# Chunk 4's last 64 keys share a bank with sums of values, in one matmul group

## The chip, the cores and the metric

The kernel runs on one core of a Trainium2 chip. The metric is the device time in microseconds; the kernel before has a median of 1121.96 us over three runs (1121.49 to 1125.24). A core has a matmul engine (TensorE, PE in the profile, with its weight loads as PEld), VectorE (DVE), ScalarE (ACT), GpSimd (POOL), and SyncE (SP), which issues the DMAs here. Matmuls write to PSUM, which has eight banks of 512 float32 columns in each of 128 partitions.

## The reference

Two stages follow each other: an attention whose mask is causal by blocks of 64, over 8 batches of 8 heads (576 positions, head size 64), and a gated feed-forward on its 4608 rows of 512 (hidden size 2048).

```python
scores = scale * np.matmul(q, k.transpose(0, 1, 3, 2))
mask = block_i >= block_j                  # blocks of 64 positions
attn = exp(scores - max); attn = attn / (sum(attn) + 1e-09)
x = np.matmul(attn, v)                     # then heads side by side: 4608 x 512
h = x @ w_in                               # 512 -> 2048
g = h * (1.0 / (1.0 + np.exp(-1.702 * h)))
out = g @ w_out                            # 2048 -> 512
```

## The kernel before

**Attention.** The kernel takes the heads two at a time: turn `n` of 32 works on pair `n`, the two heads of which lie in partitions 0 to 63 and 64 to 127. `prep` (L292) turns q and k on VectorE into `qk`. The 576 queries of a head form five chunks: chunk 0 has 64 queries, chunks 1 to 4 have 128 each, and chunk `i` sees the first 64(2i+1) keys, which is 576 for chunk 4. `score` (L305) multiplies a chunk's queries with its keys into PSUM banks, `weigh` (L340) takes masked scores out of a bank with a VectorE operation that also finds the maximum (L351) and applies the exponential on ScalarE (L358), `normalise` (L364) divides by the sum (GpSimd at L376, from turn 8 on VectorE for chunk 4 at L378), and `turn` (L382) transposes the weights on VectorE (L385, L390). After chunk 4 the turned weights are rearranged by 16 DMAs. `av` (L429) multiplies them with the values one turn later, so turn `n` holds the sums of values of pair `n`-1.

Chunk 4 is wider than a bank: 576 columns against 512. So `score` cuts its keys in two pieces, 0 to 255 and 256 to 575, each with a bank per head: four banks. With float32 each matmul shows as two records per head in the trace, and the two heads, in different halves of the array, run beside each other.

**Feed-forward.** It runs in float32r with every operand split in a high and a low part, so each product is three matmuls. A *step* of it, as the words below call it, is a tile of 384 rows with 128 of the 2048 hidden columns. Its first half is 12 matmuls into one bank (`hp`); then come the gate (tanh on ScalarE L562, a VectorE operation L563 that reads `hp` and writes `g`, a rounding on ScalarE L571, a subtraction on GpSimd L82). The second half is 9 matmuls into three banks (`acc`) and runs after the next step's first half. There is a single `hp` bank, so a first half can't begin before L563 of the step ahead of it is done.

**What sets the order.** `ORDER` (L26) has a string for each phase; its third string is for turns 9 to 31 (turn 8 has `HANDOVER`). An item is a group of chunks to score (`3+0/2+1`, `4`), `V` (the sums of values), `L` (`prep` of the next pair), or `-`. After each item, `advance` (L592) adds feed-forward steps up to a quota, from turn 9 on only whole ones, so a group of attention matmuls always stands after a first half. TensorE keeps this program order (L98, L101). On the other engines the framework's scheduler lays down a fixed order when the program is built, by data dependences and priorities (the gate has a raised one, L561 and L570), and each engine then takes its instructions strictly in that order.

Banks outside the feed-forward come from `bank()` (L89), which goes round w0 to w3 in these turns. Buffers `e0` and `e1` hold the weights of even and odd chunks.

Of the kernel before, what the change touches and what calls it, by code (L numbers as in the profile page):

```python
# [10 lines left out]
F32 = mybir.dt.float32  # L11
# [14 lines left out]
ORDER = (  # L26
# [3 lines left out]
)  # L30

START = "1+0 - B 2/3 L C - V - 4 - a - - -"
# [8 lines left out]
def attention_moe_kernel(  # L41
# [9 lines left out]
    nc = tc.nc  # L51
    B, H, S, D = q.shape
# [51 lines left out]

    ident = sp.tile([P, P], F32, name="ident")
    make_identity(nc, ident)
    MW = 448
    mask = sp.tile([P, MW], mybir.dt.bfloat16, name="mask")
    nc.gpsimd.memset(mask, 0.0)
    nc.gpsimd.memset(mask[0:BLK, MW - BLK : MW], -8e9)  # L110
# [16 lines left out]
        return home[name, g]  # L127

    xr = sp.tile([P, NDC, RING], F32, name="xr")


    vp = sp.tile([P, 2, NCH, D], F32, name="vp")
# [32 lines left out]
    def width(i):  # L165
        return BLK * (2 * i + 1)
# [125 lines left out]
    def prep(n):  # L292

        tag = "e0" if early(n) and n % 2 else "qk"
        qk[n] = d2.tile([P, 2, S], F32, tag=tag, name="qk", bufs=1)
        for x in range(2):
            nc.vector.transpose(out=qk[n][:, x], in_=raw[n][:, x].rearrange("p c d -> p (c d)"))  # L297
        raw.pop(n)
        m = follower(n)
        if m is not None:  # L300
            load(m)

    stats = {}

    def score(n, banks):  # L305

        if n not in stats:
            mx = d2.tile([P, NCH + 1, 2], F32, tag="mx", name="mx")
            sm = d2.tile([P, NCH, 2], F32, tag="sm", name="sm")
            stats[n] = (mx, sm)  # L310
        todo = []
        for chunks in banks:

            part = []
            for lo, hi in ((0, 512),) if width(chunks[0]) <= 512 else ((0, 256), (256, S)):
                ss = [bank() for _ in range(2)]
                c = 0
# [12 lines left out]
            todo.append(sorted(part, key=lambda x: (chunks[::-1].index(x[0]), x[2])))  # L330
        for chunks, part in zip(banks, todo):
            e = {}
            for i, hd, lo, hi, s in part:
                e[i] = weigh(n, i, hd, lo, hi, s, e.get(i))
            for i in chunks[::-1]:
                normalise(n, i, e[i])
                if not early(n):
                    turn(n, i, e[i])

    def weigh(n, i, hd, lo, hi, s, e):  # L340
# [10 lines left out]
        nc.vector.tensor_tensor_reduce(  # L351
            out=e[0:m, hd, lo:hi], in0=s, in1=mk,
            op0=ALU.add, op1=ALU.min, scale=-0.125,
            scalar=3e38 if lo == 0 else mx[0:m, NCH, hd : hd + 1],
            accum_out=mx[0:m, i, hd : hd + 1] if hi == w else mx[0:m, NCH, hd : hd + 1],
        )
        if hi == w:
            nc.scalar.activation(  # L358
                out=e[0:m, hd], in_=e[0:m, hd], func=AF.Exp, scale=-1.0,
                bias=mx[0:m, i, hd : hd + 1], accum_out=sm[0:m, i, hd : hd + 1],  # L360
            )
        return e
# [63 lines left out]
                in_=src[:, x : x + 2 * len(part), a : a + 2],  # L426
            )

    def av(n):  # L429

        b, h = divmod(n, HP)
        before_av(n)
        o, o0 = bank(), bank()

        todo = []
        for i in range(1, NCH):
            c = (i - 1) * P
            todo += [(o, c, P, j, pw[:, :, SLOT[i] + j]) for j in range(i)]
            todo.append((o, c + BLK, BLK, i, pw[:, 2:4, 9 + i]))
        last = len(todo) - 1  # L440
        todo.append((o0, 0, BLK, 0, pw[:, 0:2, 10]))

        for x, (bk, c, nn, j, w) in enumerate(todo):
            for hd in range(2):
                mm(
                    out=bk[hd * D : hd * D + D, c : c + nn].rearrange("d (a c) -> d a c", c=32),
                    lhsT=values(n)[:, hd, j], rhs=w[:, :, hd], start=x in (0, last + 1), stop=x >= last,
                )
        c0 = (b % 2) * S
        nc.scalar.copy(out=xr[:, h, c0 : c0 + BLK], in_=o0[:, 0:BLK])  # L450
        nc.scalar.copy(out=xr[:, h, c0 + BLK : c0 + S], in_=o)
        m = follower(n)
        if m is not None:
            load_v(m)

    def follower(n):

        m = {0: 2, 1: 3, 2: 4, 3: None}.get(n, n + 1)
        return None if m is None or m >= NPAIR else m

    def order(n):
        return {HP: START, 2 * HP: HANDOVER}.get(n, ORDER[phase(n)]).split()

    def step(n):

        turns["n"] = n
        now = n < NPAIR

        def item(x):
            if x == "V":  # L470
                return (lambda: av(n - 1)) if n else None
            if x == "L":
# [33 lines left out]
    def chunk_time(tt):  # L506
        return 4 * unit1(tt) + tt // P * 650
# [69 lines left out]
        yield from second(prev)  # L577


    ends = np.cumsum([0.0] + [NFC * chunk_time(tt) for _, tt in TILES])  # L580

    def quota(pos):
        xs, ys = zip(*TILES_BY)
        return -1.0 if pos < xs[0] else np.interp(pos, xs, [ends[y if y >= 0 else y - 1] for y in ys])

    def heads_for(t):
        return -(-sum(TILES[t]) // S) * H
# [36 lines left out]
    for n in range(NPAIR + 1):  # L624
        items = step(n)
        for sl, fn in enumerate(items):
            if fn is not None:
                fn()
            if order(n)[sl] == "V":
# [35 lines left out]
```

## Time and profile before

| | before |
|---|---|
| median of 3 runs | 1121.96 us |
| profiled execution: own time | 1120.49 us |
| profiled execution: span of the instructions | 1118.6 us |
| TensorE busy | 1076.4 us (96%) |
| VectorE busy | 583.0 us (52%) |
| ScalarE busy | 498.6 us (45%) |
| GpSimd busy | 406.7 us (36%) |
| mean granted TensorE clock | 0.992 |

Turn 8 begins at about 192 us, the last group of chunk 4 is at 947 us, and behind it the feed-forward runs alone up to 1118.6 us. In the rows of the timeline, the first number is the start in us from the span's beginning, the second the time in us, then engine, line, operation, what it writes and reads, the shape and a count. Starts of matmuls tell more than their times: the next matmul starts while the one before it still drains, so the recorded times overlap.

### The profile page before, as it was taken

What the parts mean: (1) busy time and instruction counts of PE and PEld (TensorE: products, weight loads), DVE (VectorE), ACT (ScalarE), POOL (GpSimd) and SP (SyncE); (2) the same over time, 40 slices, a digit from 0 to 9 for tenths busy, and PEclk for the clock granted to TensorE, in tenths of its full rate; (3) what the DMA queues carried; (4) which work ended last, traced back from release to release, by engine and by line L of the source; (5) the groups of instructions that cost most, each with busy time, mean ns of one, the idle gap of its engine ahead of it and who ended that gap; (6) DMA issues with size and microseconds to landing.
All of it is one profiled execution on the core that took longest, in us unless ns stands there. A gap on an engine that the chain in (4) does not pass through costs nothing. (4 is left out here: it accounts for less than half of the span.)

```text
span 1118.6 us, 19977 instructions
## 1 busy us (share of the span) xinstructions
PE 1076.4 (96%) x6960; PEld 908.7 (81%) x6960; DVE 583.0 (52%) x1856; ACT 498.6 (45%) x1321; POOL 406.7 (36%) x509
## 2 busy tenths in 40 slices
PE   5969998999999999999999999999999999999998
PEld 3757776788888888888888888888888888899997
DVE  6776885545545555654555655645545654211210
ACT  5866776434534433534443543444434444322322
POOL 4665664333333332333333333333333233122222
PEclk9979999999999999999999999999999999999999
DMA  8734532332444432343443333344342332200000
GB/s 171 205 89 153 150 73 62 84 79 57 105 86 86 103 80 64 64 98 78 98 101 74 75 93 65 70 108 85 81 107 63 71 85 58 54 29 1 29 1 29
DMA packets 219365, 91.25 MB, mean 82 GB/s; under 512 B 197760, under 2 KB 197760, under 8 KB 219264
## 3 DMA queue, kind: packets, MB, share of 16 engines
q1 hardware_dynamic: 214528, 89.38, 34.0%
q10 hardware_dynamic: 4736, 0.59, 0.3%
q8 instruction: 55, 0.90, 0.3%
q14 instruction: 46, 0.38, 0.1%
HBM read 45.09 MB, written 9.44 MB: 49 GB/s over the span
## 5 line engine op out<-in xcount | busy, mean ns | idle before, releaser
L82 POOL TENSOR_TENSOR gl<-g,gh 128x384 fp32r<-128x384 f32 x192 | 194.7, 1014 | 551.5 <-ACT gh L571 449.1
L99 PE MATMUL hp<-xh,wih 128*128 128x384 f32 x768 | 264.7, 345 | 7.9 <-DVE g L563 6.9
L563 DVE SCALAR_TENSOR_TENSOR g<-g,hp 128x384 f32<-128x384 f32 x192 | 105.9, 552 | 319.1 <-ACT g L562 317.8
L99 PE MATMUL hp<-xh,wil 128*128 128x384 f32 x768 | 258.4, 336 | 0.1
L562 ACT ACTIVATE g<-hp 128x384 f32<-128x384 f32 x192 | 94.1, 490 | 359.8 <-PE hp L99 354.8
L99 PE MATMUL hp<-xl,wih 128*128 128x384 f32 x768 | 253.9, 338 | 0.4 <-DVE xl L82 0.4
L99 PE MATMUL acc<-woh,gh 128*128 128x512 f32 x576 | 233.9, 406 | 0.0
L99 PE MATMUL acc<-wol,gh 128*128 128x512 f32 x576 | 226.9, 394 | 0.0
L99 PEld LDWEIGHTS hp<-xh,wih 128*128 128x128 f32 x768 | 144.2, 188 | 34.1 <-DVE g L563 23.1
L99 PE MATMUL acc<-woh,gl 128*128 128x512 f32 x576 | 167.9, 393 | 0.3 <-POOL gl L82 0.3
L571 ACT CAST gh<-g 128x384 fp32r<-128x384 f32 x192 | 98.4, 513 | 156.5 <-DVE g L563 156.4
L99 PEld LDWEIGHTS hp<-xh,wil 128*128 128x128 f32 x768 | 144.3, 188 | 6.5 <-POOL wil L82 0.7
L358 ACT ACTIVATE e<-e,mx 64x64 f32<-64x64 f32 (+4 forms) x240 | 132.3, 552 | 37.6 <-DVE mx L351 37.6
L376 POOL TENSOR_TENSOR e<-e,sm 64x64 f32<-64x64 f32 (+1 forms) x192 | 113.6, 612 | 95.0 <-DVE sm L371 46.5
L99 PEld LDWEIGHTS hp<-xl,wih 128*128 128x128 f32 x768 | 143.6, 188 | 1.3 <-DVE xl L82 1.3
L99 PE MATMUL bank<-qk 64*128 64x320 f32 (+4 forms) x768 | 122.5, 428 | 14.5 <-DVE qk L297 11.1
L99 PEld LDWEIGHTS acc<-woh,gh 128*128 128x128 f32 x576 | 107.9, 187 | 34.2 <-issue 10.5
L99 PEld LDWEIGHTS acc<-woh,gl 128*128 128x128 f32 x576 | 107.8, 188 | 25.9 <-POOL gl L82 1.2
L99 PEld LDWEIGHTS acc<-wol,gh 128*128 128x128 f32 x576 | 108.3, 188 | 16.7 <-POOL wol L82 0.3
L351 DVE CUSTOM_DVE_ANT_0 e<-bank,mask 64x64 f32<-64x64 f32 (+4 forms) x240 | 89.7, 417 | 56.9 <-PE bank L99 52.8
L385 DVE STREAM_TRANSPOSE turned<-e 128x384 f32<-128x384 f32 (+1 forms) x192 | 92.3, 499 | 48.8 <-POOL e L376 48.3
L99 PEld LDWEIGHTS bank<-qk 64*128 64x128 f32 x768 | 69.6, 193 | 54.2 <-issue 25.4
(50 smaller groups left out, 956.0 us busy)
## 6 DMA issues: line engine op xcount, KB each, us to landing
turned<-turned SPq DMA_DIRECT2D x192, 80.0 KB, 2.1
turned<-turned SPq DMA_DIRECT2D x96, 112.0 KB, 2.2
raw<-in_q_dram SPq DMA_DIRECT2D x128, 72.0 KB, 2.4
out_dram<-osb SPq DMA_DIRECT2D x36, 256.0 KB, 2.2
raw<-in_k_dram SPq DMA_DIRECT2D x120, 72.0 KB, 2.6
turned<-turned SPq DMA_DIRECT2D x96, 88.0 KB, 2.1
words<-in_moe_w_in_dram SPq DMA_DIRECT2D x16, 512.0 KB, 6.3
vp<-in_v_dram SPq DMA_DIRECT2D x60, 128.0 KB, 2.4
```

The costliest lines, as they stand in the source:

```text
L82: eng.tensor_tensor(out=out, in0=in0, in1=in1, op=ALU.subtract)
L99: return tc.keep_in_program_order(nc.tensor.matmul(**kw))
L351: nc.vector.tensor_tensor_reduce(out=e[0:m, hd, lo:hi], in0=s, in1=mk, op0=ALU.add, op1=ALU.min, scale=-0.125, scalar=3e38 if lo == 0 else ...
L358: nc.scalar.activation(out=e[0:m, hd], in_=e[0:m, hd], func=AF.Exp, scale=-1.0, bias=mx[0:m, i, hd : hd + 1], accum_out=sm[0:m, i, hd : hd ...
L376: nc.gpsimd.tensor_tensor(out=x, in0=x, in1=sc.to_broadcast([m, width(i)]), op=ALU.mult)
L385: nc.vector.transpose(out=tw[:, :, SLOT[i] : SLOT[i] + i, hd].rearrange("p b j c -> p j b c"), in_=e[:, hd, 0 : i * P],)
L562: nc.scalar.activation(out=g, in_=hp[:, 0:tt], func=AF.Tanh, scale=1.702)
L563: nc.vector.scalar_tensor_tensor(out=g, in0=g, scalar=1.0, in1=hp[:, 0:tt], op0=ALU.add, op1=ALU.mult)
L571: nc.scalar.copy(out=gh, in_=g)
```

## The change

- `ORDER`'s third string: `V` and `4`, which stood at items 5 and 8, become one item `V4` at item 9 of 13. So from turn 9 on, the sums of values of pair `n`-1 and chunk 4 of pair `n` are one group of matmuls with nothing between.
- That group needs four banks: two for the sums of values (`o`, `o0`), two for keys 0 to 511 of chunk 4, one per head. The last 64 keys of both heads go into columns 64 to 191 of `o0`, of which the sums of values use 64 columns. One matmul over all 128 partitions does both heads: `ends` holds the last keys of the two heads as a block diagonal with zeros elsewhere.
- `prep` writes keys 0 to 511 into `qk` and the last 64 into `ends`, by two more small transposes (for pairs 9 on).
- In `av` (all turns) chunk 0's matmuls, which fill `o0`, come first and not last.
- From turn 8 on, the weights of chunks 0 and 1 lie in a buffer of their own (`small`), no longer in `e0` and `e1`.

```diff
-    "3+0/2+1 - - - V - - 4 - - - L -",
+    "3+0/2+1 - - - - - - - V4 - - L -",
...
+    ends = sp.tile([P, 2, BLK], F32, name="ends")
+    nc.gpsimd.memset(ends, 0.0)
...
         for x in range(2):
-            nc.vector.transpose(out=qk[n][:, x], in_=raw[n][:, x].rearrange("p c d -> p (c d)"))
+            z = QC * P if x and n > 2 * HP else S
+            nc.vector.transpose(out=qk[n][:, x, 0:z], in_=raw[n][:, x, 0 : z // 32].rearrange("p c d -> p (c d)"))
+            for hd in range(2 if z < S else 0):
+                r = slice(hd * D, hd * D + D)
+                nc.vector.transpose(
+                    out=ends[r, hd], in_=raw[n][r, x, z // 32 : S // 32].rearrange("p c d -> p (c d)")
+                )
...
-            for lo, hi in ((0, 512),) if width(chunks[0]) <= 512 else ((0, 256), (256, S)):
+            cuts = (0, 512) if width(chunks[0]) <= 512 or shared is not None else (0, 256, S)
+            for lo, hi in zip(cuts, cuts[1:]):
...
+            if shared is not None:
+                i = NCH - 1
+                mm(
+                    out=shared, lhsT=qk[n][:, 0, slice(*qrange(i))], rhs=ends.rearrange("p h k -> p (h k)"),
+                    start=True, stop=True,
+                )
+                part += [(i, hd, QC * P, S, shared[:, hd * BLK : (hd + 1) * BLK]) for hd in range(2)]
...
-            e = d2.tile([P, 2, w], F32, tag=f"e{i % 2}", name="e", bufs=1)
+            if i > 1:
+                e = d2.tile([P, 2, w], F32, tag=f"e{i % 2}", name="e", bufs=1)
+            else:
+
+                if n not in small:
+                    small[n] = room("wm", [P, WC], F32, "e")
+                e = small[n][:, 2 * 3 * BLK * (1 - i) : 2 * (3 * BLK + w * (1 - i))].rearrange("p (h k) -> p h k", h=2)
...
+        todo.insert(0, (o0, 0, BLK, 0, pw[:, 0:2, 10]))
         last = len(todo) - 1
-        todo.append((o0, 0, BLK, 0, pw[:, 0:2, 10]))
...
+    def values_and_4(n):
+        o0 = bank()
+        av(n - 1, o0)
+        if n < NPAIR:
+            score(n, [[NCH - 1]], o0[:, BLK : 3 * BLK])
```

The places in the built order of which the next part speaks are these. On TensorE, turn 19: before, chunk 4 was a group between two halves of feed-forward steps.

```order
L99 MATMUL hp_5910<-xl_978,wih_187 128x384
L99 MATMUL bank_5930<-qk_5655 128x256
L99 MATMUL bank_5931<-qk_5655 128x256
L99 MATMUL bank_5934<-qk_5655 128x320
L99 MATMUL bank_5935<-qk_5655 128x320
L99 MATMUL acc0_5869<-woh_410,gh_5886 128x512
```

In the changed kernel, the same turn has the end of the sums of values (bank 5875; chunk 0's are in 5874), then chunk 4 with the shared bank.

```order
L99 MATMUL bank_5875<-turned_77,vp_75 64x128 x8
L99 MATMUL bank_5875<-turned_77,vp_75 64x64 x2
L99 MATMUL bank_5912<-qk_5636 128x512
L99 MATMUL bank_5913<-qk_5636 128x512
L99 MATMUL bank_5874<-ends_73,qk_5636 128x128
L99 MATMUL acc0_5813<-woh_412,gh_5830 128x512
```

The two groups have become one, with five matmuls behind the sums of values where four stood alone.

On VectorE, turn 19, from the last score piece of chunk 4 to the first of turn 20: before, the two transposes of `prep` (`qk`, L297, q and k) stand ahead of chunk 4's scaling (L378) and transposes (L385, L390), and the gates of the two steps behind chunk 4 (`g_5990`, `g_6031`) come last.

```order
L351 ISA e_5938,mx_5696<-bank_5935,mask_69,mx_5696 128x320
L351 ISA mx_5696 128x1
L297 STREAM_TRANSPOSE qk_5997<-raw_5658 128x576 x2
L368 TENSOR_SCALAR sm_5697<-sm_5697 128x2
L371 RECIPROCAL sm_5697<-sm_5697 128x2
L378 TENSOR_SCALAR e_5938<-e_5938,sm_5697 128x576 x2
L385 STREAM_TRANSPOSE turned_75<-e_5938 128x4x4x32 x2
L390 STREAM_TRANSPOSE turned_75<-e_5938 64x2x2x32
L563 SCALAR_TENSOR_TENSOR g_5990<-g_5990,hp_5977 128x384
L563 SCALAR_TENSOR_TENSOR g_6031<-g_6031,hp_6018 128x384
```

In the changed kernel (lines of the new file: L302 and L305 are `prep`'s transposes, L599 is the gate, L404, L411 and L416 are chunk 4's scaling and transposes), the same stretch:

```order
L302 STREAM_TRANSPOSE qk_5976<-raw_5641 128x576
L394 TENSOR_SCALAR sm_5680<-sm_5680 128x2
L397 RECIPROCAL sm_5680<-sm_5680 128x2
L404 TENSOR_SCALAR e_5917<-e_5917,sm_5680 128x576 x2
L411 STREAM_TRANSPOSE turned_77<-e_5917 128x4x4x32 x2
L599 SCALAR_TENSOR_TENSOR g_5969<-g_5969,hp_5956 128x384
L416 STREAM_TRANSPOSE turned_77<-e_5917 64x2x2x32
L305 STREAM_TRANSPOSE ends_73<-raw_5641 64x64
L599 SCALAR_TENSOR_TENSOR g_6012<-g_6012,hp_5999 128x384
L302 STREAM_TRANSPOSE qk_5976<-raw_5641 128x512
L305 STREAM_TRANSPOSE ends_73<-raw_5641 64x64
```

The transpose of k (`qk_5976` 128x512) has moved from ahead of chunk 4's scaling to behind the gate `g_6012` of the second step after chunk 4. On TensorE, that step's first half (`hp_5999`) stands right before the first scores of turn 20, which read `qk_5976`.

```order
L99 MATMUL hp_5999<-xh_979,wil_190 128x384
L99 MATMUL hp_5999<-xl_980,wih_189 128x384
L99 MATMUL bank_6021<-qk_5976 128x448
L99 MATMUL bank_6022<-qk_5976 128x448
L99 MATMUL bank_6021<-qk_5976 128x64
```

Of the 22 turns 9 to 30, twelve have the transpose of k behind the gate of the last first half before the next turn's scores, as here (13, 16, 18, 19, 20, 21, 23, 24, 26, 27, 28, 29); in the other ten it stands ahead of that gate.

More of the change, by code (lines that the diff above doesn't have):

```diff
@@ L106, in attention_moe_kernel @@
     make_identity(nc, ident)
-    MW = 448
+    MW = 576
     mask = sp.tile([P, MW], mybir.dt.bfloat16, name="mask")
@@ L303, in attention_moe_kernel, with score @@
     stats = {}
-    def score(n, banks):
+    def score(n, banks, shared=None):
         if n not in stats:
@@ L338, in score @@
                     turn(n, i, e[i])
+    small = {}
     def weigh(n, i, hd, lo, hi, s, e):
@@ L427, in flip, with av @@
             )
-    def av(n):
+    def av(n, o0=None):
         b, h = divmod(n, HP)
         before_av(n)
-        o, o0 = bank(), bank()
+        o = bank()
+        if o0 is None:
+            o0 = bank()
         todo = []
@@ L446, in av @@
                     out=bk[hd * D : hd * D + D, c : c + nn].rearrange("d (a c) -> d a c", c=32),
-                    lhsT=values(n)[:, hd, j], rhs=w[:, :, hd], start=x in (0, last + 1), stop=x >= last,
+                    lhsT=values(n)[:, hd, j], rhs=w[:, :, hd], start=x in (0, 1), stop=x in (0, last),
                 )
@@ L459, in follower @@
         return None if m is None or m >= NPAIR else m
+    def values_and_4(n):
+        o0 = bank()
+        av(n - 1, o0)
+        if n < NPAIR:
+            score(n, [[NCH - 1]], o0[:, BLK : 3 * BLK])
     def order(n):
@@ L471, in item @@
                 return (lambda: av(n - 1)) if n else None
+            if x == "V4":
+                return lambda: values_and_4(n)
             if x == "L":
@@ L577, in moe @@
         yield from second(prev)
-    ends = np.cumsum([0.0] + [NFC * chunk_time(tt) for _, tt in TILES])
+    tile_ends = np.cumsum([0.0] + [NFC * chunk_time(tt) for _, tt in TILES])
     def quota(pos):
         xs, ys = zip(*TILES_BY)
-        return -1.0 if pos < xs[0] else np.interp(pos, xs, [ends[y if y >= 0 else y - 1] for y in ys])
+        return -1.0 if pos < xs[0] else np.interp(pos, xs, [tile_ends[y if y >= 0 else y - 1] for y in ys])
     def heads_for(t):
@@ L628, in attention_moe_kernel @@
                 fn()
-            if order(n)[sl] == "V":
+            if order(n)[sl][0] == "V":
                 heads_done = 2 * n
```

## The prediction

> **What bounds the kernel now.** I read the page, then the busy times by stage, then who waits for whom on TensorE in the stage that changes, and last the timelines around the groups that move.
>
> ```profile
> PE 1076.4 (96%) x6960; PEld 908.7 (81%) x6960; DVE 583.0 (52%) x1856; ACT 498.6 (45%) x1321; POOL 406.7 (36%) x509
> ```
> ```profile
> 236.00:950.00 714.00, 708.62 (x4628) 600.88 (x4627) 392.02 (x1299) 299.46 (x807) 239.24 (x310) 1.00 0.37 82
> ```
> ```profile
> PE hp L99 <- DVE g L563: 5.1, 6, 0.9
> ```
>
> From 236 to 950 us, where turns 9 to 31 run, TensorE (first of the busy times) is busy for 708.6 of 714 us at full granted clock, and the wait view of this stretch has one entry: six waits for the gate's VectorE operation. So TensorE's chain sets the end. What the change is worth there is the matmul time it saves, the waits it removes, and the waits it makes. Other engines cost something only when TensorE waits for them. Before 236 us the order of the groups on TensorE stays, and from 950 us on it runs the feed-forward alone; I put no change there.
>
> **Term A, one group in place of two (turns 9 to 31, 23 times).** Rows of TensorE around chunk 4 and around the sums of values, turn 18:
>
> ```profile
> 526.87 0.34 PE L99 MATMUL hp<-xl,wih 128*128 128x384 f32 x1
> 527.14 1.24 PE L99 MATMUL bank<-qk 64*128 64x256 f32 x8
> ...
> 527.67 0.70 PE L99 MATMUL bank<-qk 64*128 64x320 f32 x4
> ...
> 527.94 0.44 PE L99 MATMUL bank<-qk 64*128 64x320 f32 x2
> ...
> 528.31 0.50 PE L99 MATMUL acc<-woh,gh 128*128 128x512 f32 x1
> 528.65 0.39 PE L99 MATMUL acc<-wol,gh 128*128 128x512 f32 x1
> ```
> ```profile
> 515.54 2.99 PE L99 MATMUL bank<-turned,vp 128*64 128x128 f32 x60
> 518.45 0.50 PE L99 MATMUL acc<-woh,gh 128*128 128x512 f32 x1
> 518.79 0.40 PE L99 MATMUL acc<-wol,gh 128*128 128x512 f32 x1
> 519.03 0.39 PE L99 MATMUL acc<-woh,gh 128*128 128x512 f32 x1
> ```
>
> Starts tell the cost. The last 384-column matmul holds the next start off by 0.27 us (526.87 to 527.14), where within a half they follow each other after 0.18 (further below, eleven of them from 502.68 to 504.70): 0.10 to enter a group, rounded up. The first matmul behind a group takes 0.34 (528.31 to 528.65, 518.45 to 518.79) against 0.24 for the next (518.79 to 519.03): 0.10. A pass over 320 columns takes 0.27 (527.67 to 527.94), 0.84 ns per column, both heads side by side. Chunk 4 has two passes over 576 columns, 0.97 us, but lasts 1.17 (527.14 to 528.31): 0.20 more, a second weight load that nothing covers and the drain at the end. The values' group lasts 2.91 us with its own drain.
>
> Before, a turn spends 0.10 + 2.91 + 0.10 on V and 0.10 + 1.17 + 0.10 on chunk 4: 4.48 us. After, 0.10 + 2.91, then two passes of 512 columns (0.86) with 0.20 as before, then the shared matmul's two passes of 128 (0.22). For the shared matmul's second load and the step back to the feed-forward no row exists: nothing at the cheapest, 0.25 at the dearest (0.10 twice and 0.05). I take 0.07, nearer to the low end, since the feed-forward has the same 128 by 128 shape. Sum 4.36: 0.12 less, 2.8 us in 23 turns, with bounds of 4.4 saved and 1.4 lost.
>
> Two sentences of the Trainium skill stand beside this. Its page "TensorEngine Tiling (Array Packing)", section "Key Properties", says that a change of tiling mode drains the engine; the rows agree (0.10 on entry), and by that rule alone the way back costs nothing, which would make the saving 4.4 us. Its page "TensorE: Matmul & The Clock Gate", Part 3 on packing small matmuls, says that matmuls in different row groups run at once and that one over all rows takes as long as a small one; it speaks against this change, since 128 columns at full height take the place of 64 side by side, 0.11 us a turn or 2.5 us in all by the pass row above.
>
> **Term B, the wait for the gate behind chunk 4 goes.** Two turns, early and late, and an undisturbed half for comparison:
>
> ```profile
> 244.19 0.86 PE L99 MATMUL acc<-woh,gl 128*128 128x512 f32 x3
> 245.88 0.45 PE L99 MATMUL hp<-xh,wih 128*128 128x384 f32 x1 [0.82 <-DVE g L563]
> ```
> ```profile
> 501.82 0.86 PE L99 MATMUL acc<-woh,gl 128*128 128x512 f32 x3
> 502.68 0.45 PE L99 MATMUL hp<-xh,wih 128*128 128x384 f32 x1
> ```
> ```profile
> 519.95 0.84 PE L99 MATMUL acc<-woh,gl 128*128 128x512 f32 x3
> 520.62 0.33 PE L99 MATMUL hp<-xh,wih 128*128 128x384 f32 x1
> ```
>
> Undisturbed, the half starts 0.67 us after the three matmuls begin; in the early turn after 1.69, in the late one after 0.86. So six early turns lose 1.0 us each and some fifteen late ones 0.19 (with about 0.05 more at the half ahead of chunk 4): 9.6 us in all. The reason stands on VectorE, where chunk 4's chain is ahead of the gate (turn 17; chunk 4 starts on TensorE at 494.98):
>
> ```profile
> 494.98 0.49 PE L99 MATMUL bank<-qk 64*128 64x256 f32 x2
> ```
> ```profile
> 495.71 0.42 DVE L351 CUSTOM_DVE_ANT_0 e<-bank,mask 128x256 f32<-128x256 f32 x1 [3.09 <-PE bank L99]
> ...
> 496.87 0.55 DVE L351 CUSTOM_DVE_ANT_0 e<-bank,mask,mx 128x320 f32<-128x320 f32 x1
> ...
> 497.81 1.43 DVE L297 STREAM_TRANSPOSE qk<-raw 128x576 f32<-128x576 f32 x2
> 499.17 0.13 DVE L368 TENSOR_SCALAR sm<-sm 128x2 f32<-128x2 f32 x1
> ...
> 500.40 1.30 DVE L385 STREAM_TRANSPOSE turned<-e 128x512 f32<-128x512 f32 x2
> 501.73 0.31 DVE L390 STREAM_TRANSPOSE turned<-e 64x128 f32<-64x128 f32 x1
> 502.07 0.55 DVE L563 SCALAR_TENSOR_TENSOR g<-g,hp 128x384 f32<-128x384 f32 x1
> ```
> ```profile
> 497.46 0.78 ACT L358 ACTIVATE e<-e,mx 128x576 f32<-128x576 f32 x1 [0.30 <-DVE mx L351]
> ```
> ```profile
> L351 DVE CUSTOM_DVE_ANT_0 e<-bank,mask 128x448 f32<-128x448 f32 x48 | 27.7, 610 | 0.0
> ```
>
> I rebuild this chain for the changed order, counting from the group's first score matmul. The first score operation comes at 0.73 now, and at 0.73 + 0.43 = 1.16 with 512 columns (two passes of 256 more). 256 columns take 0.42, 448 take 0.61: about 1 ns a column, so 512 take 0.67 and follow each other after 0.60; the 64-column piece is 0.27 (0.55 less 256 columns). The first exponential starts 0.05 behind the end of its head's last piece: 1.16 + 1.20 + 0.27 + 0.05 = 2.68. From there to the sums (L368) it is 1.71 (497.46 to 499.17): 4.39. From the sums to the gate it is 2.90, less the 0.34 of L390, which the new order puts behind the gate: gate from 6.95 to 7.50. TensorE would begin that half, without a wait, at 502.68 - 494.98 - 0.19 = 7.51 now, and at 7.6 behind the longer group. So the gate is just in time. The moved transposes of `prep` fill VectorE's wait for the exponentials, and the gate of the step before runs beside the 2.9 us of V. I take 8.0 us saved, with 1.6 left for what is late by a hair; bounds are 3 (the chain 0.3 longer each turn) and 9.6.
>
> **Term C, a new wait: the first scores of the next turn.** The order shows it: in 12 of 22 turns the transpose of k stands behind the gate of the half that runs right before the scores that read it. Before, that transpose was done far ahead (497.81 in the turn above, seven us before the scores). The price comes from the rows at such a place:
>
> ```profile
> 504.70 0.34 PE L99 MATMUL hp<-xl,wih 128*128 128x384 f32 x1
> 504.97 2.11 PE L99 MATMUL bank<-qk 64*128 64x448 f32 x16
> ```
> ```profile
> 505.13 0.49 ACT L562 ACTIVATE g<-hp 128x384 f32<-128x384 f32 x1 [1.97 <-PE hp L99]
> ```
> ```profile
> 505.65 0.56 DVE L563 SCALAR_TENSOR_TENSOR g<-g,hp 128x384 f32<-128x384 f32 x1 [3.04 <-ACT g L562]
> ```
> ```profile
> L385 DVE STREAM_TRANSPOSE turned<-e 128x512 f32<-128x512 f32 x48 | 31.1, 687 | 0.0
> ```
> ```profile
> 57.88 0.75 DVE L297 STREAM_TRANSPOSE qk<-raw 128x576 f32<-128x576 f32 x1
> ```
> ```profile
> 58.69 0.43 PE L99 MATMUL bank<-qk 64*128 64x192 f32 x2 [2.52 <-DVE qk L297]
> ```
>
> The half's last matmul starts at 504.70 and the scores at 504.97. The tanh can't start before 505.13, the gate before 505.65; it ends at 506.21, a 512-column transpose (0.69, the nearest form) at 506.90, and TensorE goes on 0.06 behind such a transpose (58.63 to 58.69): 506.96. That is 1.99 late, or 1.90 if the two VectorE operations overlap as others do by 0.09. VectorE idles 3 us before this gate, so nothing shortens it, and behind the waiting scores stand all later matmuls, since TensorE keeps its order. 12 times 1.95 is **23.4 us lost**. The bounds are 19.5 (two of the twelve places harmless) and 26 (2.2 us each, should another 0.2 lie between the links); TensorE waits for nothing else there that could hide it.
>
> **Term D, small moves.** In turn 16 the new order has three transposes of GpSimd-scaled weights ahead of the first gate behind the scores.
>
> ```profile
> L376 POOL TENSOR_TENSOR e<-e,sm 128x448 f32<-128x448 f32 x48 | 43.8, 933 | 14.2 <-DVE sm L371 13.5 <-ACT e L358 0.7
> L376 POOL TENSOR_TENSOR e<-e,sm 128x320 f32<-128x320 f32 x48 | 33.6, 720 | 29.1 <-DVE sm L371 29.1
> L376 POOL TENSOR_TENSOR e<-e,sm 128x192 f32<-128x192 f32 x48 | 23.3, 507 | 33.9 <-ACT e L358 33.9
> ```
> ```profile
> 509.28 1.83 POOL L376 TENSOR_TENSOR e<-e,sm 128x448 f32<-128x448 f32 x2 [0.47 <-DVE sm L371]
> ```
>
> Two of each are 4.3 us. Before, the first began 4.3 us behind the scores' start (504.97 to 509.28); with the scores of chunks 1 and 2 now ahead of its sums on VectorE I take 5.0. With a transpose (0.31) and the gate (0.55) the bank is free at 10.2; TensorE needs it behind the scores (2.1) and three halves of 2.1, at 8.4: 1.8 us lost, once. The two extra transposes per turn and the DMAs for the next pair, which SyncE issues behind the transpose of k, have most of a turn (some 30 us) to land in, so they cost nothing unless that shrinks below the time of a transfer.
>
> **Sum.** -2.8 - 8.0 + 23.4 + 1.8 = +14.4 us on the profiled execution's 1120.5 (span 1118.6), so 1134.9. The median shown is 1.5 above that execution: **1136.5 us**.
>
> **Rivals.** (1) *Faster: the wait of term C is not paid.* If the scores wait less than (2.8 + 8.0 - 1.8) / 12 = 0.75 us a turn, the kernel gains; at nothing it comes to 1113. For it: the trace of before has no such wait. Against: VectorE takes instructions in the order of the rows, and the gate needs a half that TensorE has only just finished. (2) *The gains cancel it:* the wait at 0.75 us gives 1122, no change; it needs most of the 12 places to be harmless. (3) *Term B brings nothing,* the chain being 0.35 longer than I rebuilt: 1144.5. (4) *The shared matmul waits for ScalarE,* which must first copy chunk 0's sums out of the same bank (the order has that copy ahead of the gate's rounding, some 3 us before it is needed). If it came late by 0.5 us a turn, 1148.
>
> **How the numbers follow.** Forecast 0.68; rival 1 0.12; rival 2 0.06; rival 3 0.08; rival 4 0.06. A measurement tells about 0.3% (3.4 us) from no change. Slower holds the forecast and rivals 3 and 4, 0.82; within 0.3% 0.06; faster 0.12. The range leaves out rival 1 below, and what is dearer than 1147 above: 1124 to 1147.
>
> **What would show it.** In the new profile, TensorE should wait for `qk` (L302) about 12 times for 1.5 to 2 us each between 330 and 900 us, and the six waits for the gate should be gone; the group V with chunk 4 should last about 4.2 us. I am wrong if the wait view has no entry for `qk`, if the time stays under 1124, or if waits for ScalarE stand at the shared matmul.

## The result, and the profile after

| kernel | median us (range, runs) | against the kernel before, 95% interval |
|---|---|---|
| before | 1123.60 (1121.49 to 1125.28, 4) | |
| changed | 1139.72 (1139.47 to 1140.05, 4) | 1.0148 [1.0128, 1.0168] |

The changed kernel is slower by 1.5%, 16 us; its profiled span is 1138.1 us where that of before is 1118.6. The forecast of 1136.5 us lies 3.2 us below the median.

The page's first part (busy time, share of the span, instructions) and the windows view of the stretch with turns 9 to 31 in the changed kernel:

```profile
PE 1075.2 (94%) x6914; PEld 915.9 (80%) x6914; DVE 597.6 (53%) x1902; ACT 500.9 (44%) x1321; POOL 403.6 (35%) x510
```
```profile
236.00:970.00 734.00, 708.66 (x4665) 609.64 (x4664) 407.28 (x1346) 302.96 (x811) 236.84 (x310) 1.00 0.36 80
```

TensorE has no more work than before (1075 us against 1076), and in this stretch as much busy time as before (708.7 against 708.6 us), but the stretch holds 25 us in which it idles, where there were 5.4. What it waits for is in the wait view of the same stretch (who waits for whom: us in all, times, longest):

```profile
PE bank L99 <- DVE qk L302: 23.8, 12, 2.2
PE hp L99 <- DVE g L599: 1.4, 1, 1.4
```

The six waits for the gate have become one, and twelve waits for the transpose of k have come in. One of the twelve, ahead of turn 17, in the timeline (start, duration, engine, instruction, idle time before it and its releaser):

```profile
476.48 0.34 PE L99 MATMUL hp<-xl,wih 128*128 128x384 f32 x1
476.91 0.49 ACT L598 ACTIVATE g<-hp 128x384 f32<-128x384 f32 x1 [1.47 <-PE hp L99]
477.43 0.56 DVE L599 SCALAR_TENSOR_TENSOR g<-g,hp 128x384 f32<-128x384 f32 x1 [2.42 <-ACT g L598]
477.90 0.71 DVE L302 STREAM_TRANSPOSE qk<-raw 128x512 f32<-128x512 f32 x1
478.76 1.51 PE L99 MATMUL bank<-qk 64*128 64x448 f32 x10 [1.94 <-DVE qk L302]
```

From the half's last matmul to the scores it is 478.76 - 476.48 = 2.28 us, where 0.27 is the step without a wait: 2.01 us lost. VectorE did nothing for 2.42 us ahead of the gate; the transpose needed nothing of it and only stood behind it.

How far the changed kernel is behind the one before, by the start of each turn's first scores in the two traces:

| turn | 4 | 6 | 7 | 8 | 9 | 16 | 17 | 24 | 31 | end |
|---|---|---|---|---|---|---|---|---|---|---|
| us behind | 1.7 | 0.5 | 4.8 | 6.6 | 6.6 | 2.4 | 6.0 | 13.1 | 20.3 | 19.5 |

Two things stand in it. From turn 10 on the kernel gains 0.4 to 1.2 us in a turn without the wait, and loses 1.0 to 2.1 net in a turn with it (3.6 in turn 16). And 6.6 us were lost before turn 9, where I had put no change.

### The profile page after: what moved, and what is told of

It reads as the page before. It is cut to its first block, busy times and chain, and to the rows that moved or that the text cites. A ratio compares the mean times of both kernels' runs of the same rounds, so it can differ in the third digit from the quotient of the medians.

```text
span 1138.1 us, 19974 instructions
## 1 busy us (share of the span) xinstructions
PE 1075.2 (94%) x6914; PEld 915.9 (80%) x6914; DVE 597.6 (53%) x1902; ACT 500.9 (44%) x1321; POOL 403.6 (35%) x510
## 4 chain that ended last, share of the span: by engine, by line
PE 50%; DVE 3%; DMA 2%; ACT 2%; issue 1%; SPq 1%; POOL 0%; POOLq 0%; DVEq 0%; ACTq 0%
PE hp L99 21%; PE acc L99 21%; PE bank L99 9%; DMA turned<-turned 2%; ACT e L384 1%; SPq L423 1%; DMA vp<-in_v_dram 1%; DVE e L404 1%; DVE qk L302 1%; DVE g L599 1%; DVE turned L411 1%; DVE e L377 0%; DVE sm L394 0%; DVE sm L397 0%; ACT g L598 0%
## 5 line engine op out<-in xcount | busy, mean ns | idle before, releaser
L599 DVE SCALAR_TENSOR_TENSOR g<-g,hp 128x384 f32<-128x384 f32 x192 | 105.5, 549 | 372.6 <-ACT g L598 372.2
L99 PE MATMUL bank<-qk 64*128 64x320 f32 (+5 forms) x676 | 119.3, 454 | 37.0 <-DVE qk L302 31.0
L377 DVE CUSTOM_DVE_ANT_0 e<-bank,mask 64x64 f32<-64x64 f32 (+5 forms) x240 | 103.2, 463 | 56.2 <-PE bank L99 55.8
L99 PEld LDWEIGHTS bank<-qk 64*128 64x128 f32 x676 | 62.3, 194 | 70.3 <-issue 46.5
L99 PEld LDWEIGHTS bank<-turned,vp 128*64 128x64 f32 x1800 | 86.9, 139 | 13.1 <-issue 6.4
```

What stands on the lines that cost most here:

```text
L99: return tc.keep_in_program_order(nc.tensor.matmul(**kw))
L377: nc.vector.tensor_tensor_reduce(out=e[0:m, hd, lo:hi], in0=s, in1=mk, op0=ALU.add, op1=ALU.min, scale=-0.125, scalar=3e38 if lo == 0 else ...
L599: nc.vector.scalar_tensor_tensor(out=g, in0=g, scalar=1.0, in1=hp[:, 0:tt], op0=ALU.add, op1=ALU.mult)
```

## The experiments

Ten kernels ran. Numbers in brackets are the 95% interval of the ratio to the kernel before, whose median in these comparisons was 1123.2 to 1123.6 us.

| run | median us (range) | ratio | behind the kernel before at turn 9 / 31, us |
|---|---|---|---|
| 1 k ahead | 1123.8 (1119.9 to 1126.0) | 1.0006 [0.9993, 1.0020] | 9.5 / 6.4 |
| 2 early order | 1138.2 (1133.3 to 1140.9) | 1.0128 [1.0095, 1.0161] | 1.1 / 19.9 |
| 3 pins only | 1163.0 (1162.0 to 1164.9) | 1.0356 [1.0333, 1.0379] | 8.4 / 42.7 |
| 4 both | 1117.2 (1116.6 to 1119.1) | 0.9947 [0.9930, 0.9963] | 2.6 / -0.6 |
| 5 before, chunk 0 first | 1132.2 (1132.0 to 1134.1) | 1.0080 [1.0066, 1.0094] | 11.8 / 11.8 |
| 6 more waits taken out | 1114.0 (1113.1 to 1116.2) | 0.9915 [0.9901, 0.9930] | 1.2 / -5.3 |
| 7 shared matmul twice | 1121.5 (1118.6 to 1123.6) | 0.9984 [0.9973, 0.9995] | -0.3 / -1.2 |
| 8 groups apart, 4 turns | 1119.8 (1117.2 to 1120.0) | 0.9959 [0.9944, 0.9974] | 2.7 / 0.4 |
| 9 groups apart | 1117.9 (1116.0 to 1119.0) | 0.9949 [0.9934, 0.9964] | -0.2 / -3.8 |
| 10 gate later | 1122.2 (1121.7 to 1124.9) | 0.9993 [0.9981, 1.0005] | 1.3 / 3.2 |

### 1. The transpose of k ahead of the last gate

```diff
-    "3+0/2+1 - - - - - - - V4 - - L -",
+    "3+0/2+1 - - - T - - - V4 - - L -",
...
+            if z < S:
+                tc.keep_in_program_order(d)
...
+                    if turns["n"] > 2 * HP:
+                        tc.keep_in_program_order(d)
```

`d` is the transpose of k in the first place and the gate's VectorE operation in the second; a third pin, not shown here, is on the transpose of chunk 4's tail. The scheduler may no longer exchange these. `T` issues the transposes of the turn's scaled weights at that slot, and `L` the transpose of chunk 4's tail with its DMAs, so that the other operations keep their places.

> The changed kernel with one thing moved: in every turn from the tenth on, the transpose of the next pair's k stands ahead of the gate of the turn's last half on VectorE (chunk 4's turned transposes and its tail's transpose with its 16 DMAs go to other places in the turn, so that the rest of VectorE's order stays). Theory (the late transpose of k is the loss): the waits of TensorE for qk (L302) after 236 us, 24.7 us in 12 turns by the starts, go and nothing takes their place: 1139.7 - 24.7 = 1115, between 1112 and 1119. Rival (the wait only moves: the scores, or a half shortly behind, then wait for the gate or for another VectorE operation): 1130 or more, with a new entry of 1 us a turn in the waits.

Measured 1123.8, between the two. The wait view from 236 us on:

```profile
PE hp L99 <- DVE g L627: 4.8, 3, 2.1
PE bank L99 <- DVE qk L302: 3.5, 2, 1.7
```

Ten of the twelve waits are gone. Two are left, where VectorE has four other operations ahead of the transpose (run 6). By starts, 24.7 us of waits for qk have become 3.6. Against this stand two halves that wait longer (turn 9 by 1.4, turn 13 by 1.65 us, both of this edit's order), 2.9 us that this run lost by turn 9 beside the changed kernel, and 3.4 us at half clock in turn 9, which cost 1.7. All halves together are 2.8 us later. From the changed kernel's span this makes 1138.1 - 21.1 + 2.8 + 2.9 + 1.7 = 1124.4 us, and the span of this run is 1124.2. So the waits were on the path, and their removal was paid in full; I had counted as if none were left and none came.

### 2 and 5. Chunk 0's matmuls last or first in the early turns

Run 2 is the changed kernel with this in `av`; run 5 is the kernel before with the reverse.

```diff
-        todo.insert(0, (o0, 0, BLK, 0, pw[:, 0:2, 10]))
+        first = (o0, 0, BLK, 0, pw[:, 0:2, 10])
...
+        if n < 2 * HP:
+            todo.append(first)
...
+        else:
+            todo.insert(0, first)
```

> The changed kernel, in which the sums of values of the first eight pairs again have chunk 0's matmuls last, as before the change. Theory (the 6.5 us that the changed kernel had lost by turn 8 come from this order, through the engines behind it): 1139.7 - 6.5 = 1133, between 1131 and 1135. Rival (they come from where stretches of half clock happened to fall in the first 210 us, and the order of these matmuls is worth nothing): 1139 to 1141.

> The kernel before, in which the sums of values of the first eight pairs have chunk 0's matmuls first, as in the changed kernel; nothing else of the change is in it. Theory (this order alone makes the early loss: it was worth 6.6 us between the runs with k's transpose ahead): 1123.2 + 6 = 1129, between 1127 and 1132, and in the trace turn 9's scores start about 5 us later than before. Rival (the loss is of other stretches of the run, or of where half clock falls by chance): 1122 to 1125.

Run 2's trace is 5.4 us ahead of the changed kernel's at turn 9, but its time does not tell: four executions took 1133.3 to 1140.9 us, and their median of 1138.2 lies between the two expectations. Its profile lost 5 us again later. The same wait for qk, ahead of turn 14's scores, in the changed kernel and in run 2, in the timeline and in the windows view of two stretches each (the third number from the right is the granted clock):

```profile
383.81 2.11 PE L99 MATMUL bank<-qk 64*128 64x448 f32 x16 [1.94 <-DVE qk L302]
```
```profile
379.18:382.59 3.41, 2.68 (x14) 2.06 (x13) 2.55 (x7) 1.00 (x2) 1.01 (x1) 1.00 0.10 22
382.59:386.00 3.41, 2.19 (x17) 1.60 (x18) 2.31 (x10) 1.25 (x6) 0.99 (x1) 1.00 0.64 153
```
```profile
378.35 3.79 PE L99 MATMUL bank<-qk 64*128 64x448 f32 x16 [1.94 <-DVE qk L302]
```
```profile
375.15:378.56 3.41, 1.47 (x10) 1.18 (x10) 2.44 (x6) 1.00 (x2) 0.82 (x2) 1.00 0.36 85
378.56:381.98 3.42, 3.42 (x16) 2.18 (x14) 1.54 (x9) 1.39 (x7) 0.64 (x1) 0.50 0.57 134
```

The wait is the same, but in run 2 the scores behind it took 3.79 us and not 2.11: the clock had fallen to half for 3.4 us (1.7 us lost). It happened behind three of run 2's twelve waits and behind none of the changed kernel's. So a wait of 2 us can cost 1.7 more.

The traces show where the difference lies. In all twelve, the granted clock changes only at the edges of a fixed grid of 3.413 us. The grid falls on other places of the kernel's work in each execution; the stretches above are pieces of it. In run 2 the three waits each fall whole into one piece (3.41 - 1.47 = 1.94 us idle). An edge cuts the other nine, and all twelve of the changed kernel, and leaves at most 1.78 us idle in a piece (0.73 and 1.22 here). From 236 to 970 us, in all traces, the clock was at half behind every piece with 1.94 us idle or more and behind none with 1.78 or less. Before 236 us idle time alone does not sort them: the clock fell behind pieces with as little as 1.14 us idle, and stayed up behind one with 1.97.

Run 5 settles that the order alone is a loss: it makes the kernel before 9 us slower, a little more than expected. Up to 187 us TensorE, ScalarE and VectorE start their operations in the same order in run 5 as in the changed kernel, while VectorE's order in the kernel before differs from it in many places, the first at 81 us. The two are about as far behind at turn 8's scores, 6.7 and 6.6 us. The other 5.1 us of run 5's trace come in turn 8, where the changed kernel loses nothing. The stretch of turn 8 in the kernel before and in run 5:

```profile
200.00:230.00 30.00, 29.61 (x150) 24.49 (x149) 14.13 (x46) 11.94 (x32) 9.87 (x13) 1.00 0.43 103
```
```profile
200.00:230.00 30.00, 25.22 (x155) 21.65 (x155) 15.55 (x52) 12.08 (x33) 8.85 (x12) 0.89 0.20 54
```

TensorE idles 4.8 us of 30 there instead of 0.4, and the clock is at 0.89. Most of it is one wait, ended by a score's operation on VectorE, with the clock at half behind it, so that the sums of values take 5.60 us. In the kernel before, the same operation held up only the last four matmuls, chunk 0's; the other 56 had started at 195.05:

```profile
199.44 0.34 PE L99 MATMUL bank<-turned,vp 128*64 128x64 f32 x4 [1.52 <-DVE mx L351]
```
```profile
206.59 5.60 PE L99 MATMUL bank<-turned,vp 128*64 128x64 f32 x60 [4.32 <-DVE mx L351]
```

From turn 8's scores to this operation VectorE's order is the same in both traces. With chunk 0 first, the whole group stands behind the wait of chunk 0's matmuls, whose bank this operation frees. The changed kernel has its first new wait of over a microsecond in turn 6, and the clock is at half right behind it:

```profile
153.22 0.80 PE L99 MATMUL bank<-qk 64*128 64x320 f32 x2 [1.14 <-DVE mx L377]
```
```profile
150.00:170.00 20.00, 17.72 (x93) 13.73 (x92) 15.27 (x44) 13.87 (x36) 12.19 (x14) 0.91 0.11 38
```

Over all traces, turn 8's scores start at 191.0 to 195.5 us in the eight kernels with chunk 0 last in the early pairs, and at 197.6 to 200.5 in the four with chunk 0 first; there is no overlap. How much of the loss is waiting and how much the clock was not tried apart. By turn 9 the changed kernel had spent 30.7 us at half clock and the one before 17.1; half of the difference, 6.8, is about the whole loss. But run 4 had spent 30.7 too and was only 2.6 behind, so this is no rule.

### 3. Only the two pins

```diff
+            if z < S:
+                tc.keep_in_program_order(d)
...
+                    if turns["n"] > 2 * HP:
+                        tc.keep_in_program_order(d)
```

The changed kernel with the two pins of run 1 and nothing else moved by hand.

> The changed kernel with the transpose of k ahead of the last gate in all turns, but in the order that the scheduler then makes, three or four transposes of GpSimd-scaled weights stand ahead of the first gate behind the scores in some 21 turns, as in turn 16 of the changed kernel. It puts term D to the test at scale. Theory (each such turn costs what turn 16 shows, 1.5 us at a half that waits for its bank, and the waits for qk are gone): 1139.7 - 24.7 + 21 x 1.5 = 1146.5, between 1141 and 1152. Rival (turn 16's loss was no matter of this order): 1115.

Measured 1163.0: the direction of the theory, 11 us over its range. The wait view from 236 us on, and one of the turns:

```profile
PE hp L99 <- DVE g L601: 32.9, 25, 4.6
```
```profile
536.98 1.01 DVE L418 STREAM_TRANSPOSE turned<-e 64x128 f32<-64x128 f32 x3
539.04 0.31 DVE L418 STREAM_TRANSPOSE turned<-e 64x128 f32<-64x128 f32 x1 [1.05 <-POOL e L404]
539.38 0.56 DVE L601 SCALAR_TENSOR_TENSOR g<-g,hp 128x384 f32<-128x384 f32 x1
539.99 0.44 PE L99 MATMUL hp<-xh,wih 128*128 128x384 f32 x1 [1.18 <-DVE g L601]
```

The gate waits for a transpose that waits for GpSimd, and TensorE for the gate: 1.35 us by the starts in most turns, near the 1.5 I had put, so term D's mechanism is a cost. Not foreseen were 0.25 at the half behind chunk 4 in nearly every turn (5 us in all; run 10 shows why), one loss of 4.8 us in turn 9, and two stretches of half clock behind such waits (from 237.6 and 398.0 us, 6.8 us in all), which cost 3.4.

### 4. Both together

The edits of runs 1 and 2.

> The first and the second of these together: k's transpose ahead of the gate, and chunk 0's matmuls last in the first eight pairs. Theory (two separate losses): 1139.7 - 24.7 - 6.5 = 1108.5, between 1105 and 1112, which is below the kernel before (1123.6) by about 15. Rival (the early 6.5 us are not of this order): 1115, as the first one alone.

Measured 1117.2. It beats both kernels, by less than I wrote: what run 1 left over is left here too, and its waits are the same to 0.01 us. Against run 1 it gains 6.6 us, all of it before turn 9 by the table above, which is the theory's price for the early order.

### 6. Three more of the waits

```diff
-        return {HP: START, 2 * HP: HANDOVER}.get(n, ORDER[phase(n)]).split()
+        return {HP: START, 2 * HP: HANDOVER, 21: SPLIT, 29: SPLIT}.get(n, ORDER[phase(n)]).split()
...
-                    if turns["n"] > 2 * HP:
+                    if turns["n"] > 2 * HP + 1:
...
+                    if turns["n"] in (21, 29):
+                        tc.keep_in_program_order(d)
```

`SPLIT` has `L` one slot earlier; the last `d` is the subtraction that makes `xl`. The second change leaves the gates of turn 9 unpinned again.

> The faster kernel of the runs so far (k's transpose ahead, chunk 0's matmuls last in the early pairs) with three of its remaining waits taken away by order alone: in turns 21 and 29 the transpose of k stands ahead of the four subtractions that wait for the roundings of the next tile (1.8 us each at the scores of turns 22 and 30), and turn 9 has the gates unpinned again (2.3 us at a half, of which the changed kernel had 0.9). Theory (those waits are on TensorE's chain): 1117.2 - 3.6 - 1.4 = 1112.2, between 1110 and 1114.5. Rival (the subtractions, now behind the gate, hold the next tile's first half, whose matmuls read them): 1116 to 1119, with waits for xl at the halves behind the scores of turns 22 and 30.

Measured 1114.0, inside the theory's range, 9 us faster than the kernel before. No wait for qk is left (wait view from 236 us):

```profile
PE hp L100 <- DVE g L637: 5.2, 4, 1.5
```

But of the two times 1.8 us that went, 1.5 came back each time at a half behind those scores, which now waits for its gate. The rival had the place right, and not the operation that is waited for. Turn 9 brought more: its halves wait 0.9 us and no longer 2.3, and the 3.4 us of half clock that followed them in run 4's trace are gone.

### 7. The shared matmul twice

```diff
-                mm(
-                    out=shared, lhsT=qk[n][:, 0, slice(*qrange(i))], rhs=ends.rearrange("p h k -> p (h k)"),
+                for _ in range(2):
+                    mm(
+                        out=shared, lhsT=qk[n][:, 0, slice(*qrange(i))], rhs=ends.rearrange("p h k -> p (h k)"),
```

> The faster kernel of the runs so far with the shared matmul (64 columns of chunk 4 at full height) issued twice in each turn, the second time over the first with the same result. Theory of term A (its price is its columns, two passes of 128 at 0.84 ns a column, with weight loads covered): the group from the last 384-column start to the first behind it grows from 4.49 us by 0.21 to 0.22, and the time by 23 x 0.22 = 4.9 to 1122. Rival (its weight load stands open each time, as at the change to the feed-forward): 0.3 to 0.42 a turn, 1124 to 1127. Second rival (it runs beside the passes ahead of it): under 0.1 a turn, 1117 to 1119.

Measured 1121.5, 4.4 more than run 4. In its timeline:

```profile
490.72 0.34 PE L99 MATMUL hp<-xl,wih 128*128 128x384 f32 x1
490.99 2.98 PE L99 MATMUL bank<-turned,vp 128*64 128x64 f32 x60
493.90 1.13 PE L99 MATMUL bank<-qk 64*128 64x512 f32 x4
494.96 0.71 PE L99 MATMUL bank<-ends,qk 128*128 128x128 f32 x4
495.43 0.48 PE L99 MATMUL acc<-woh,gh 128*128 128x512 f32 x1
```

From 490.72 to 495.43 it is 4.71 us; with one shared matmul it is 4.49 in all turns. The second costs 0.22, its columns and no weight load.

### 8 and 9. The two groups apart again

```diff
-    "3+0/2+1 - - - T - - - V4 - - L -",
+    "3+0/2+1 - - - T - V - 4 - - L -",
```

Run 8 had `V` one slot ahead of `4`, run 9 as shown, two; the bank of the shared columns is held from the one to the other.

> The faster kernel of the runs so far with the sums of values one slot earlier, so that a slot of feed-forward stands between them and chunk 4 with its shared matmul: two groups again, everything else in place. Theory of term A (a group costs 0.10 on entry and 0.10 at the first matmul behind it, whatever is in it): 0.20 to 0.30 more a turn, 22 turns, so 1117.2 + 4.4 to 6.6 = 1121.6 to 1124, between 1120 and 1126. Rival (joining the groups is worth nothing, the engine drains between values and chunk 4 all the same): 1116 to 1118.5. Second rival (the gate behind chunk 4 has less cover and is waited for, as in the kernel before): another 0.2 a turn, 1126 to 1130, with that wait in the starts of the halves.

> Again the first of the faster kernels (1117.2) with the sums of values in a group of their own, now two slots earlier, so that a step of feed-forward stands between them and chunk 4 in every turn (one slot earlier, only 4 of 23 turns had one between). Theory of term A (0.10 on entry and 0.10 at the first matmul behind a group, whatever is in it; the four turns that had two groups took about 0.20 more by their starts): 0.20 x 22 = 4.4 more, 1121.6, between 1120 and 1124. Rival (joining is worth nothing): 1116 to 1118.5. Second rival (a gate is waited for as in the kernel before): 0.2 a turn more, 1126 or above.

Run 8's time answers nothing: in 19 of 23 turns no feed-forward step came between, so the group stayed one. Run 9, in the timeline:

```profile
487.90 0.34 PE L99 MATMUL hp<-xl,wih 128*128 128x384 f32 x1
488.17 2.99 PE L99 MATMUL bank<-turned,vp 128*64 128x64 f32 x60
491.09 0.50 PE L99 MATMUL acc<-woh,gh 128*128 128x512 f32 x1
...
495.19 0.34 PE L99 MATMUL hp<-xl,wih 128*128 128x384 f32 x1
495.46 1.13 PE L99 MATMUL bank<-qk 64*128 64x512 f32 x4
496.52 0.49 PE L99 MATMUL bank<-ends,qk 128*128 128x128 f32 x2
496.76 0.47 PE L99 MATMUL acc<-woh,gh 128*128 128x512 f32 x1
```

From the last 384-column start to the matmul behind the group it is 3.19 and 1.57 us. One ordinary step of 0.17 is counted twice in that, and the first matmul behind the values takes 0.10 more than the next: 3.19 + 1.57 - 0.17 + 0.10 = 4.69, against 4.49 for one group. So joining is worth 0.20 us a turn. The time, 1117.9, falls into the rival's range, but for another reason: in this order the two waits for qk that run 4 kept (3.6 us) are gone, and with 21 turns in which the groups are apart, 1117.2 - 3.6 + 21 x 0.20 = 1117.8. I should have seen that the order of VectorE moves with `V`.

### 10. How much room term B has

```diff
-        if i == NCH - 1 and n > 2 * HP:
-            tail.append((n, i, e))
-        else:
-            turn_tail(n, i, e)
+        turn_tail(n, i, e)
```

On run 6: the transpose of chunk 4's tail stands ahead of the gate again.

> The fastest kernel of the runs so far (1114.0) with the 0.31 us transpose of chunk 4's tail ahead of the gate in every turn, where chunk 4's chain in the kernel before had it. It measures how much room term B leaves: the gate behind chunk 4 ends at 631.36 in the trace of the kernel with both edits, and the half that needs its bank starts at 631.64, unwaited; behind a gate that is waited for, TensorE goes on 0.05 after it, so the room is 0.23. Theory (the prediction's 'just in time'): 0.31 - 0.23 = 0.08 a turn, some 20 turns, +1.6: 1115.6, between 1114 and 1117.5, and halves behind chunk 4 that start 0.03 to 0.1 later. Rival (the wait of the kernel before comes back whole): 0.2 or more a turn, 1118 or above. Second rival (there is more room than the rows show): 1114, no half later.

Measured 1122.2, the rival's side. The gate in run 4 (run 6 has the same times to 0.01 us) and in run 10, with the matmuls around it:

```profile
629.61 1.30 DVE L421 STREAM_TRANSPOSE turned<-e 128x512 f32<-128x512 f32 x2
...
630.84 0.52 DVE L634 SCALAR_TENSOR_TENSOR g<-g,hp 128x384 f32<-128x384 f32 x1
630.95 0.85 PE L99 MATMUL acc<-woh,gl 128*128 128x512 f32 x3
631.38 0.31 DVE L434 STREAM_TRANSPOSE turned<-e 64x128 f32<-64x128 f32 x1
...
631.64 0.33 PE L99 MATMUL hp<-xh,wih 128*128 128x384 f32 x1
```
```profile
503.63 0.31 DVE L432 STREAM_TRANSPOSE turned<-e 64x128 f32<-64x128 f32 x1
503.64 0.86 PE L100 MATMUL acc<-woh,gl 128*128 128x512 f32 x3
503.97 0.55 DVE L634 SCALAR_TENSOR_TENSOR g<-g,hp 128x384 f32<-128x384 f32 x1
...
504.58 0.44 PE L100 MATMUL hp<-xh,wih 128*128 128x384 f32 x1
```

Against the three matmuls, the gate ends at +0.41 in run 4 and at +0.88 in run 10: 0.47 later, not 0.31. The gate had overlapped the transposes ahead of it by 0.07, and behind the extra one it doesn't. The half starts at +0.69 and +0.94. So the room was 0.47 - 0.25 = 0.22, as I had read it, and the step that failed is the transpose's price. By starts the halves are 5.4 us later than in run 6, 19 of them by 0.26, and a wait of 1.96 us with 3.4 us of half clock behind it has 1.7 of the other 2.8.

## Why the prediction came out right, and where it did not

By the starts in the two traces, beside the terms put:

| term | put | measured | by |
|---|---|---|---|
| A, one group | -2.8 | -2.1 | 23 x 0.093 |
| B, waits behind chunk 4 | -8.0 | -8.6 | 10.3 us of late halves, now 1.7 without turn 16 |
| C, transpose of k behind the gate | +23.4 | +24.7 | ten of 2.01, two of 2.26 |
| D, turn 16 | +1.8 | +1.5 | one half, late by 1.54 |
| before turn 9 | 0 | +6.6 | start of turn 9's scores |
| not in any term | 0 | -2.6 | spacing in the halves and the end |
| sum | +14.4 | +19.5 | spans 1138.1 - 1118.6 |

**C** is the change's loss. It was read from the order (12 places) and from three links of the trace (the half's end, the gate, a transpose), and each was paid: 12 of 12. That it is the path, and not a sign of something else, run 1 shows: with only this order undone the time fell by 16 us, and by starts the waits gave back 21. The two of 2.26 are those where ScalarE rounds the next tile ahead of the gate's tanh, a hair over the 2.2 of my upper bound.

**B** held: the gate came in time but for turns 9 and 16, and was late by 0.24 twice. Run 10 shows both that this gate is what the halves wait for and how little was between: 0.2 us.

**A** held in its parts, with a smaller saving. In the changed kernel:

```profile
497.44 0.34 PE L99 MATMUL hp<-xl,wih 128*128 128x384 f32 x1
497.71 2.98 PE L99 MATMUL bank<-turned,vp 128*64 128x64 f32 x60
500.62 1.13 PE L99 MATMUL bank<-qk 64*128 64x512 f32 x4
501.68 0.49 PE L99 MATMUL bank<-ends,qk 128*128 128x128 f32 x2
501.92 0.48 PE L99 MATMUL acc<-woh,gh 128*128 128x512 f32 x1
502.24 0.40 PE L99 MATMUL acc<-wol,gh 128*128 128x512 f32 x1
```

2.91 for V and 1.06 for the two passes are as put; the shared matmul takes 0.24, and the first matmul behind it 0.32 where the next takes 0.23, so 0.08 of the 0.10 of a change is still paid though both sides are 128 by 128. Together 0.33 where I had put 0.22 + 0.07. Joining saves 0.20 (run 9), chunk 4's new form takes 0.11 of it back (1.57 against 1.44 us for the group, less 0.03 at the first matmul behind). The Trainium skill's page "TensorEngine Tiling (Array Packing)", section "Key Properties", ties the drain to a change of tiling mode; by it alone this step back would be free and term A 4.4 us, and the rows do not agree. Its page "TensorE: Matmul & The Clock Gate", Part 3, has matmuls in different row groups run at once. By the prediction's 0.84 ns per column and pass, the 64 columns of both heads side by side would take 0.11 us, an estimate; run 7's 0.22 is twice that.

**D** was of the right size, and run 3 shows its mechanism in nearly every turn, at 1.35 us. Turn 16 itself was not undone alone.

**The failed step** is the sentence that before 236 us "the order of the groups on TensorE stays" and that I put no change there. The groups do stay. But the order inside them does not (chunk 0 first), and with it VectorE's order moved, in a stretch where TensorE waits for other engines anyway. Undone, it gives 6.6 us (run 4 against run 1); put into the kernel before it costs 9 (run 5), of which some 5 lie in turn 8, where the changed kernel does not pay them. That the forecast stayed near is in part luck: this miss and the 2.6 us that no term holds, together with small errors in the terms, add to 5 us of the span, and the medians differ by less than the spans (16.1 against 19.5 us: the profiled execution of before, 1120.5 us, lies 3.1 below the median of its runs).

Of the rivals, none came: the wait was paid (1, 2), B brought what it should (3), and no wait for ScalarE stands at the shared matmul (4).

**What stays open:** why the clock falls before 236 us behind stretches with so little idle time, and how the early loss divides between waits and clock. That the scheduler puts the transpose of k late because of when it takes the raw loads to land was not tried.

## What to carry to other kernels

A group that is moved takes its neighbours' order on other engines with it: list, for each wait that the path will meet next, what now stands ahead of the operation that ends it. An operation that needs nothing new (here a transpose of loaded data) costs its whole chain when it is queued behind one that does; moving it ahead, with two more pins and new slots for its neighbours, took back the loss of 16 us (run 1), and with the early order and three waits more the kernel gained 6 and 9 us (runs 4 and 6). The two pins alone, which let the scheduler move the neighbours, made it a loss of 40 (run 3). And look at the order in stretches that the change seems not to touch, above all where the bounding engine isn't yet full.

## What the runs showed of the hardware

- Leaving a group over a matmul of the same 128 by 128 shape saves little: in the medians over all turns, the first matmul behind takes 0.314 us against 0.337 behind the sums of values (128 by 64) and 0.23 for an ordinary one.
- A wait of 2 us can bring on 3.4 us of half clock directly behind it, far inside the run, at a further 1.7 us. It did so behind three of twelve like waits in run 2 and behind none in the changed kernel: the clock changes only on a grid of 3.413 us, and in run 2 those three waits (1.94 us) lay whole in one piece of it, where an edge cut the others. The Trainium skill's page "TensorE: Matmul & The Clock Gate", Part 1, has the same length, 3.4 us, for a window that must pass idle before the clock falls; here 2 us of idle time were enough.
- A gate directly behind a pair of long transposes overlapped them by 0.07 us; with a third, short transpose between, its start moved by 0.44 us though that transpose takes 0.31.
